# The block around the engines' instructions, and the order of elements in the forward width evictions

## The chip, the cores and the metric

One core of one Trainium2 chip. The metric is the device time of one execution in microseconds (us); the median of three runs stands for the kernel. TensorE (PE) multiplies matrices out of SBUF into PSUM, ScalarE (ACT) and VectorE (DVE) copy and transform, GpSimd (POOL) makes small vectors and issues some DMAs, SyncE (SP) issues most DMAs. The engines run on their own and meet only at semaphores.

## The reference

The input `x` is 2048 x 640 in bf16. It is normalised row by row, and two branches of the result are added to it.

```
xn = layernorm(x)                                  # over the 640
A  = irfft2( rfft2(xn) * (w_r + i w_i) )           # a spectral filter over both axes
B  = gelu(xn @ w1 + b1) @ w2 + b2                  # 640 -> 1536 -> 640
out = x + A + B
```

## The kernel before

**Branch B** is two dense layers on TensorE. The first layer's sums are evicted by ACT with the GELU (line 778) into `gT`; the second layer reads `gT` and `W2`. Their matmuls fill the time in which branch A waits for evictions.

**Branch A** writes the two-dimensional transform as matrix products with constant tables. In order: a fold of the rows on DVE, a transform over the first part of the long axis (PSUM into `XV`), the *forward width transform* (`XV` times `etab`, in six groups of two or three blocks, `GROUPS`), a small transform over the rest of the long axis (`Xb` times `mtab`, out into `Y`), the filter on DVE (`T`, `Z`, lines 845 and 849), and the same way back: `Z` times `ntab` into `U`, `T` or `gtab`, a DMA transpose into `XV`, the *inverse width transform* (`XV` times `getab`, out into `Wf`), an unfold on DVE (lines 900 and 905) and the last matmuls with `htab`, whose sums DVE adds up (line 961) and SyncE stores (line 964).

**The forward width transform** of a group with n blocks fills four PSUM banks: in each bank n runs of 160 sums, one bank for each of the four combinations of even and odd columns and of real and imaginary part. Two instructions evict them, v = 0 from the first two banks and v = 1 from the last two, into `Xb` as bf16. In `Xb` the sums of a block's two banks lie in turn, element by element: 320 neighbours from `v * (KP + 1)` on, with KP = 322. The helper `copy` emits an ACT activation (recorded at line 563) or a DVE copy (line 564). All matmuls are emitted by the helper at line 552.

**The order of the work** is written out by hand. `ORDER` lists for each engine the numbers of its operations one after another, and a planner (`Sched.schedule`) assigns PSUM banks and buffers along that list with a table of estimated costs. `Sched.sync` derives the semaphore waits that are needed, and `Sched.emit` gives each engine its list. The forward width transforms, the small transforms and the way back take turns in banks 0 to 3 (`ZONE`), the dense layers use banks 4 to 7.

**The emission** goes through a block: `nc.Block()` opens one, `block.sync(run("sp"))` and its four sisters each write one engine's instructions into a body of that block, and leaving the `ExitStack` closes it. On SyncE the list ends with waits for all stores (lines 440 to 442). The rows of the closing block are recorded at line 493, where the `with ExitStack()` of the kernel stands; those of the program's set-up at line 989.

Of the kernel before, what the change touches and what calls it, by code (L numbers as in the profile page):

```python
# [16 lines left out]
Q4 = 160  # L17
KP = 322
# [83 lines left out]
def dve_us(n, rate=1.0):  # L102
    return 0.066 + n / 960.0 / rate


def act_us(n, ptr=0):
    return 0.067 + n / 1200.0 + 0.078 * ptr
# [113 lines left out]
class Sched:  # L221
# [6 lines left out]
    def op(self, engs, prio, emit, reads=(), writes=(), after=(), rows=None, gate=(), alts=None, late=0.0):  # L228
        o = Op()
        o.name = writes[0].name if writes else ""  # L230
        o.engs, o.prio, o.emit = engs, prio, emit
        o.reads, o.writes, o.after = list(reads), list(writes), list(after)
        o.gate = gate if isinstance(gate, list) else list(gate)
        o.rows, o.late = rows, late
        o.nbytes = rows is not None
        o.alts, o.alt = alts, None
        o.seq = len(self.ops)
        o.eng, o.done, o.inc, o.count, o.sem = None, False, False, None, None
        o.deps = [w for b in o.reads for w in b.writers] + list(after)
        for b in o.reads:  # L240
            b.readers.append(o)
        for b in o.writes:
            b.writers.append(o)
        self.ops.append(o)
        return o
# [171 lines left out]
    def emit(self, es, last):  # L417
        nc = self.nc
        sems = {e: nc.alloc_semaphore(f"s_{e}") for e in self.engines if e != "sp"}
        for e in self.engines:  # L420
            n = 0
            for o in self.order[e]:
                if o.nbytes:
                    o.sem, o.count = nc.alloc_semaphore(f"d_{o.seq}"), 16
                elif o.inc:
                    n += 1
                    o.sem, o.count = sems[e], n
        block = es.enter_context(nc.Block())

        def run(name):  # L430
            def go(e):
                for o in self.order[name]:
                    for d in o.waits:
                        e.wait_ge(d.sem, d.count)
                    ins = o.emit(e, name) if o.alts is None else o.emit(e, o.alt)
                    if o.nbytes:
                        ins.then_inc(o.sem, 16)
                    elif o.inc:
                        ins.then_inc(o.sem, 1)
                if name == "sp":  # L440
                    for o in last:
                        e.wait_ge(o.sem, o.count)
            return go
        block.sync(run("sp"))
        block.gpsimd(run("pool"))
        block.vector(run("dve"))
        block.scalar(run("act"))
        block.tensor(run("pe"))


BLOCKS = [(0, 2), (2, 2), (4, 2), (6, 2), (8, 4), (12, 4)]
# [19 lines left out]
def bass_parallel_sum__spectral_gfnet__dense_activation_gelu__prompt_kernel(  # L471
# [21 lines left out]
    with ExitStack() as es:  # L493
        def sb(name, shape, dtype=BF):
            return es.enter_context(nc.sbuf_tensor(name, shape, dtype))

        def view(t, off, dims):
            width = int(np.prod(t.shape[1:]))
            return bass.AP(tensor=t, offset=off, ap=[[width, 128]] + dims)

        def part(t, p0, n, off, dims):
            width = int(np.prod(t.shape[1:]))
            return bass.AP(tensor=t, offset=p0 * width + off, ap=[[width, n]] + dims)
# [24 lines left out]
        xb3 = sb("Xb", [128, 6 * 2 * KP])  # L528
# [10 lines left out]
        def psb(slot, dims, off=0, p0=0, n=128):  # L539
            return bass.AP(tensor=PS, offset=p0 * 4096 + slot * 512 + off, ap=[[4096, n]] + dims)  # L540
# [15 lines left out]
        def pe(segs, prio, lst, **kw):  # L556

            return K.op([("pe", sum(u for _, u in segs))], prio, mms(lst), alts=[segs], **kw)

        def copy(dst, src, scale=1.0):  # L560
            def f(e, name):
                if name == "act":
                    return e.activation(dst(), src(), ACT.Copy, scale=scale)  # L563
                return e.tensor_copy(dst(), src())  # L564
            return f
# [32 lines left out]
        def load_w1(j, q="sp"):  # L598
# [6 lines left out]
             reads=[B_one], writes=[B_id])  # L605
# [62 lines left out]
        for c0, n in [(c, 1) for c in range(4)] + [(c, 2) for c in range(4, 16, 2)]:  # L668
            pr = 100 - c0 / 2
            B_mv, B_r = Buf(f"mv{c0}"), Buf(f"r{c0}")  # L670
            for c in range(c0, c0 + n):
                B_st = Buf(f"st{c}")
                for h in range(2):
                    st_op[c] = K.op([("dve", 0.393)], pr, lambda e, _, c=c, h=h: e.bn_stats(stats[:, c, 6 * h:6 * h + 6], view(X, c * D + H2 * h, [[1, H2]])),  # L674
                         reads=[B_x[c]], writes=[B_st], gate=mv_ops[:1])
# [3 lines left out]
                 reads=[B_mv, B_mh], writes=[B_r] + B_rs[a:b])  # L679

        for pair in range(8):
# [10 lines left out]
            for n in range(2):  # L692
# [5 lines left out]
                for d0, d1, bx in zip(cuts, cuts[1:], B_xs):  # L698
                    o = K.op([("dve", 0.066 + (d1 - d0) / 1980.0)], pr, lambda e, _, c=c, n=n, xnv=xnv, d0=d0, d1=d1: e.tensor_scalar(  # L699
                        out=xnv(n, d0, [[1, d1 - d0]]), in0=view(X, c * D + d0, [[1, d1 - d0]]), scalar1=mv[:, c, 0:1], scalar2=rstd[:, c:c + 1], op0=ALU.subtract, op1=ALU.mult),  # L700
                        reads=[B_x[c], B_rs[c]], writes=[xn, bx])
# [3 lines left out]
                if c in BYDMA:  # L705
                    ring_ops.append(K.op([("sp", 1.3)], 500, lambda e, _, c=c, n=n, xnv=xnv: e.dma_start_transpose(xnT[:, c, :, :], xnv(n, 0, [[1, D]])),
                         reads=[B_xn, xn], writes=[B_xnT[c]], rows=(40, 256)))
# [4 lines left out]
                for j0, j1, engs in ((0, 2, ["act"]), (2, 5, ["dve"])) if c < 2 else ((0, 5, ["dve", "act"]),):  # L712
# [8 lines left out]
                    if not c + j0:  # L721
# [5 lines left out]
                         reads=[tps], writes=[B_xnL[c][j0] if c < 2 else B_xnT[c]])  # L727
# [4 lines left out]
            for k, op in enumerate((ALU.add, ALU.subtract)):  # L732
                for o_, o0, o1, w in ((128 * k, 0, H2 - 1, 128), (512 + 32 * k, 128, H2 - 129, 32)):
                    ring_ops.append(K.op([("dve", dve_us(4 * w, 2))], pr, lambda e, _, op=op, x1v=x1v, xfv=xfv, o_=o_, o0=o0, o1=o1, w=w: e.tensor_tensor(  # L734
                        out=xfv(o_, [[D, 2], [2 * w, 2], [1, w]]), in0=x1v(o0, [[D, 2], [H2, 2], [1, w]]), in1=x1v(o1, [[D, 2], [H2, 2], [-1, w]]), op=op),
                        reads=[x1], writes=[xf]))
            aps = Buf(f"aps{pair}", psum, 3, ZONE["aps"])
            for n in range(2):
# [3 lines left out]
                    reads=[xf, B_g], writes=[aps])  # L742
                ring_ops.append(o)
                a_ops.append(o)
            for js in [[int(j) for j in g] for g in XASPLIT[pair].split()]:
# [3 lines left out]
                     reads=[aps], writes=[B_xa[pair]])  # L749
# [3 lines left out]
        for bi, (c0, nt) in enumerate(BLOCKS):  # L753
            for fc in range(NFC):
# [4 lines left out]
                if bi:  # L759
                    hps, at, part_ = Buf(f"hps{c0}_{fc}", psum, 1, ZONE["hps"]), 0, []  # L760
                    for js in ((0, 1, 2), (3, 4)):
                        part_ = [pe([("128", len(js) * mm_us(128 * nt))], pr + 0.01 * len(part_), lambda c0=c0, nt=nt, fc=fc, hps=hps, js=js: [
                            (psb(hps.slot, [[1, 128 * nt]]), view(W1, F * j + 128 * fc, [[1, 128]]), xnT[:, c0:c0 + nt, j, :], j == 0, j == 4) for j in js],
                            reads=B_w1s + B_xnT[c0:c0 + nt], writes=[hps], gate=part_)]
                        l1_ops += part_
                        l1_of.setdefault(bi, []).extend(part_)
                else:
                    at = 256 * (fc % 2)
                    if not at:
                        hps, part_ = Buf(f"hps0_{fc}", psum, 1, ANY), []  # L770
                        for j in range(5):
                            for t0, t1 in ((0, 1), (1, 2)) if j < LONE else ((0, 2),):
                                part_.append(pe([("128", 2 * mm_us(128 * (t1 - t0)))], pr + 8 - j - 2 * t0, lambda fc=fc, hps=hps, j=j, t0=t0, t1=t1: [
                                    (psb(hps.slot, [[1, 128 * (t1 - t0)]], 256 * h + 128 * t0), view(W1, F * j + 128 * (fc + h), [[1, 128]]), xnT[:, t0:t1, j, :], j == t0 == h == 0, j == 4) for h in range(2)],
                                    reads=[B_w1s[j]] + [B_xnL[t][j] for t in range(t0, t1)], writes=[hps], gate=part_[:1]))
# [4 lines left out]
                    reads=[hps, B_b1c], writes=[bg])  # L780
# [7 lines left out]
        def five(slot, n, lhs, tab):  # L788
            main, rem = width(slot, n, lhs, tab)
            return [(a, b, c, k % n == 0, False) for k, (a, b, c) in enumerate(main)] + [(a, b, c, False, True) for a, b, c in rem]  # L790

        def five_segs(n, far=0.0):
            return [("128", 4 * n * mm_us(Q4)), ("32", n * 0.07 + 0.02 + far)]
# [5 lines left out]
        for gi, (c0, n) in enumerate(GROUPS):  # L799
            xb = Buf(f"xb{gi}", p_xb)  # L800
            bps = Buf(f"bps{gi}", psum, 4, ZONE["bps"])
            pb_ops.append(pe(five_segs(n), PRIO["pb"] - c0 / 10, lambda c0=c0, n=n, bps=bps: five(
                bps.slot, n, lambda i, g, p0, k: part(XV, p0, k, 2048 * g + 128 * (c0 + i), [[1, 128]]), etab),
                reads=B_xa + [B_e], writes=[bps, xb]))
            for i in range(n):
                B_xb[c0 + i] = xb
                xb_at[c0 + i] = lambda xb=xb, i=i: (xb.slot * 3 + i) * 2 * KP
            for v in range(2):
                K.op([("dve", dve_us(320 * n) + 0.05), ("act", act_us(320 * n) + 0.08 * n)], PRIO["pb"] - c0 / 10,
                     copy(lambda v=v, xb=xb, n=n: view(xb3, xb.slot * 6 * KP + v * (KP + 1), [[2 * KP, n], [1, 2], [2, Q4]]),  # L810
                          lambda v=v, bps=bps, n=n: psb(bps.slot + 2 * v, [[Q4, n], [512, 2], [1, Q4]])), reads=[bps], writes=[xb])
        zone = {f"b{gi}": o for gi, o in enumerate(pb_ops)}
        for P in range(4):
            two = (2 * P, 2 * P + 1)
# [3 lines left out]
            for r in range(2):  # L818
# [6 lines left out]
                    reads=in_xb + [B_xbpad, B_m], writes=[cps])  # L825
# [16 lines left out]
            for pair, Y, TB, Z in zip(two, Ys, TBs, Zs):  # L842
                pr = PRIO["filt"] - pair / 5
                for k in range(2):
                    filt_ops.append(K.op([("dve", dve_us(4 * KP, 2))], pr, lambda e, _, k=k, Y=Y, TB=TB, pair=pair: e.tensor_tensor(  # L845
                        out=view(TT, TB.slot * 8 * KP + k * 4 * KP, [[2 * KP, 2], [KP, 2], [1, KP]]), in0=yv(Y, k == 1), in1=wv(pair, k), op=ALU.mult),
                        reads=[Y, B_wpad] + (B_w if pair == 7 else [B_w[k]]), writes=[TB], after=ring_ops))
# [4 lines left out]
            for v in range(2):  # L852
# [7 lines left out]
                for pp, U in enumerate(Us):  # L860
                    def evac(e, name, U=U, v=v, uv=uv, dps=dps, pp=pp):
                        for o_, w in ((0, 128), (512, 32)):
# [3 lines left out]
                         reads=[dps], writes=[U, B_us[pp]], after=a_ops + ring_ops)  # L866
# [10 lines left out]
        for q0, q1 in ((0, 12), (12, 16)):  # L877
            K.op([("dve", dve_us(128 * (q1 - q0))), ("act", act_us(128 * (q1 - q0)))], PRIO["eps"],
                 copy(lambda q0=q0, q1=q1: view(Yb, 8 * q0, [[128, 16], [1, 8 * (q1 - q0)]]), lambda q0=q0, q1=q1: view(XV, 4 * 2048 + 128 * q0, [[1, 16], [16, 8 * (q1 - q0)]])),
                 reads=B_v[q0:q1], writes=[B_xr], after=filt_ops)  # L880
# [7 lines left out]
        for gi, (c0, n) in enumerate(GROUPS):  # L888
# [5 lines left out]
                reads=B_v + [B_ge, B_xr], writes=[eps_], gate=[fin_ops[c0 - 5]] if c0 > 8 else [])  # L894
# [4 lines left out]
            for k, op in enumerate((ALU.add, ALU.subtract)):  # L899
# [3 lines left out]
                    reads=[yo], writes=[y2])  # L903
            for k, op in enumerate((ALU.add, ALU.subtract)):
# [3 lines left out]
                    reads=[y2], writes=[yf])  # L908
            for i in range(n):
# [26 lines left out]
                def second(c, fps, o0, w, pr, gate, base=base):  # L936
                    part_ = []
                    for f0 in range(0, NFC, 3):
# [8 lines left out]
                     reads=[xb2], writes=[xo], rows=(8, "acc"))  # L947
# [6 lines left out]
                for o0, w in [(0, D)] if c < 15 else [(0, H2), (H2, Q4), (H2 + Q4, Q4)]:  # L954
# [5 lines left out]
                        reads=[yf, B_h], writes=[fps, B_f], gate=part_ + ([l1_ops[-1]] if kept else []))  # L960
# [4 lines left out]
                                     reads=[os_, B_o], rows=(8, w * 2 if w * 2 in ROW_NS else 1280)))  # L965
# [38 lines left out]
```

## Time and profile before

| | |
|---|---|
| median of 3 runs | 147.75 us (147.56 to 147.98) |
| profiled execution, its own time | 148.03 us |
| its span, first to last recorded instruction | 146.1 us |
| PE busy / DVE / ACT / POOL | 140.2 / 112.7 / 80.9 / 23.7 us |
| granted TensorE clock | 1.0 |

The span is what the trace covers. The profiled execution's own time is 1.9 us longer; no row tells of that rest. In the rows below, a line begins with the kernel's line, the engine and the operation, then what is written and read, then how often, the busy time and the mean of one in ns; "idle before" and "<-" name what ended the wait. `PEld` is TensorE's weight load, which runs beside the matmuls. An engine's name with a q is its sequencer: waits, branches, drains and DMA issues, which do not count as busy.

### The profile page before, as it was taken

What the parts mean: (1) busy time and instruction counts of PE and PEld (TensorE: products, weight loads), DVE (VectorE), ACT (ScalarE), POOL (GpSimd) and SP (SyncE); (2) the same over time, 40 slices, a digit from 0 to 9 for tenths busy, and PEclk for the clock granted to TensorE, in tenths of its full rate; (3) what the DMA queues carried; (4) which work ended last, traced back from release to release, by engine and by line L of the source; (5) the groups of instructions that cost most, each with busy time, mean ns of one, the idle gap of its engine ahead of it and who ended that gap; (6) DMA issues with size and microseconds to landing.
All of it is one profiled execution on the core that took longest, in us unless ns stands there. A gap on an engine that the chain in (4) does not pass through costs nothing.

```text
span 146.1 us, 4081 instructions
## 1 busy us (share of the span) xinstructions
PE 140.2 (96%) x1702; PEld 90.8 (62%) x1720; DVE 112.7 (77%) x235; ACT 80.9 (55%) x145; POOL 23.7 (16%) x40
## 2 busy tenths in 40 slices
PE   7999999999999999999999999999999999999993
PEld 7788998888465455446544645554446666556572
DVE  1999999999844449789966967992422998998982
ACT  3208999999989769763555633216376755201000
POOL 2330302206100009220100120000063700000000
PEclk9999999999999999999999999999999999999999
DMA  4999999999997875949446571444559885103234
GB/s 110 320 407 354 320 132 303 150 182 241 283 162 149 193 192 123 235 99 180 94 92 121 63 154 30 40 110 94 90 116 230 175 202 180 45 4 137 90 135 135
DMA packets 30873, 23.63 MB, mean 162 GB/s; under 512 B 20488, under 2 KB 26888, under 8 KB 30728
## 3 DMA queue, kind: packets, MB, share of 16 engines
q1 hardware_dynamic: 28432, 17.81, 52.4%
q0 software_dynamic: 2368, 5.57, 17.4%
q8 instruction: 13, 0.21, 0.6%
q14 instruction: 4, 0.03, 0.1%
q10 hardware_dynamic: 56, 0.01, 0.0%
HBM read 13.55 MB, written 2.62 MB: 111 GB/s over the span
## 4 chain that ended last, share of the span: by engine, by line
PE 91%; DVE 4%; issue 2%; DMA 2%; POOL 0%
PE ps L552 90%; DVE stats L674 2%; DMA X<-in_A_x_dram 2%; DVE T L699 1%; DVE mv L676 0%; DVE xnT L564 0%; POOL rstd L678 0%; PE ps L718 0%; DVE W L961 0%
## 5 line engine op out<-in xcount | busy, mean ns | idle before, releaser
L552 PE MATMUL ps<-xnT,W 128*128 128x256 bf16 (+2 forms) x384 | 58.7, 300 | 0.2 <-DVE mv L676 0.2
L552 PE MATMUL ps<-W,gT 128*128 128x512 bf16 (+3 forms) x380 | 55.7, 292 | 1.6 <-issue 1.1
L552 PEld LDWEIGHTS ps<-W,gT 128*128 128x128 bf16 x396 | 30.3, 98 | 23.5 <-issue 1.6
L552 PEld LDWEIGHTS ps<-xnT,W 128*128 128x128 bf16 x384 | 33.3, 98 | 16.3 <-issue 1.6
L778 ACT ACTIVATE gT<-ps,b1col 128x256 bf16<-128x256 f32 (+1 forms) x72 | 35.3, 557 | 6.8 <-PE ps L552 6.5
L674 DVE BATCH_NORM_STATS2 stats<-X 128x6 f32<-128x320 bf16 x32 | 13.9, 475 | 2.2 <-DMA X<-in_A_x_dram 2.2
L563 ACT ACTIVATE Wf<-ps 128x960 bf16<-128x960 f32 (+1 forms) x8 | 7.0, 901 | 13.5 <-PE ps L552 13.5
L946 POOL DMA_DIRECT2D X<-in_A_x_dram x8 | 7.1, 1067 | 40.1 <-DMA Wf<-in_A_w_r_dram 17.6
L845 DVE TENSOR_TENSOR T<-Y,Wf 128x1288 bf16<-128x1288 bf16 x16 | 12.7, 826 | 0.0
L946 POOL DMA_DIRECT2D xnT<-in_A_x_dram x8 | 7.4, 1151 | 25.3 <-ACT xnT L928 25.3
L678 POOL TENSOR_TENSOR rstd<-mv,mhalf 128x2 f32<-128x2 f32 (+1 forms) x10 | 7.2, 715 | 26.8 <-DVE mv L676 26.7
L563 ACT ACTIVATE Xb<-ps 128x960 bf16<-128x960 f32 (+1 forms) x7 | 7.7, 1102 | 6.8 <-PE ps L552 6.8
L564 DVE CAST Y<-ps 128x644 bf16<-128x644 f32 x8 | 6.5, 828 | 5.5 <-PE ps L552 5.5
L563 ACT ACTIVATE XV<-ps 128x1280 bf16<-128x1280 f32 (+3 forms) x10 | 9.5, 961 | 0.7 <-PE ps L552 0.7
L564 DVE CAST Xb<-ps 128x960 bf16<-128x960 f32 (+1 forms) x5 | 5.9, 1176 | 4.1 <-PE ps L552 4.1
L734 DVE TENSOR_TENSOR T<-T 128x512 bf16<-128x512 bf16 (+1 forms) x32 | 8.5, 311 | 0.0
L699 DVE TENSOR_SCALAR T<-X,mv,rstd 128x640 bf16<-128x640 bf16 (+2 forms) x17 | 7.1, 430 | 0.9 <-POOL rstd L678 0.6
L900 DVE TENSOR_TENSOR Wf<-Wf 128x960 bf16<-128x960 bf16 (+1 forms) x12 | 7.0, 597 | 0.5 <-ACT Wf L563 0.3
L961 DVE TENSOR_TENSOR W<-ps,X 128x640 bf16<-128x640 f32 x8 | 6.5, 820 | 1.1 <-PE ps L552 1.1
L849 DVE TENSOR_TENSOR Z<-T 128x644 bf16<-128x644 bf16 x16 | 7.1, 487 | 0.1
L961 DVE TENSOR_TENSOR W<-ps,xnT 128x640 bf16<-128x640 f32 (+2 forms) x10 | 6.7, 685 | 0.7 <-PE ps L552 0.7
L552 PE MATMUL ps<-etab,XV 32*128 32x160 bf16 (+1 forms) x128 | 7.2, 232 | 0.0
(55 smaller groups left out, 132.3 us busy)
## 6 DMA issues: line engine op xcount, KB each, us to landing
X<-in_A_x_dram POOLq DMA_DIRECT2D x8, 320.0 KB, 4.8
xnT<-in_A_x_dram POOLq DMA_DIRECT2D x8, 320.0 KB, 5.0
out_dram<-W SPq DMA_DIRECT2D x15, 160.0 KB, 1.8
X<-in_A_x_dram SPq DMA_DIRECT2D x7, 320.0 KB, 7.5
W<-in_B_w_dram SPq DMA_DIRECT2D x5, 384.0 KB, 6.1
W<-in_B_w_dram SPq DMA_DIRECT2D x4, 480.0 KB, 7.5
Wf<-in_A_w_i_dram SPq DMA_DIRECT2D x6, 160.5 KB, 5.8
Wf<-in_A_w_r_dram SPq DMA_DIRECT2D x6, 160.5 KB, 4.1
```

Source lines behind the costliest of these rows:

```text
L552: ins = e.matmul(o_, lhsT=lw, rhs=rh, start=st, stop=sp_, skip_group_check=True)
L563: return e.activation(dst(), src(), ACT.Copy, scale=scale)
L564: return e.tensor_copy(dst(), src())
L674: st_op[c] = K.op([("dve", 0.393)], pr, lambda e, _, c=c, h=h: e.bn_stats(stats[:, c, 6 * h:6 * h + 6], view(X, c * D + H2 * h, [[1, H2]]) ...
L678: K.op([("pool", 0.65)], 500, lambda e, _, a=a, b=b: e.tensor_tensor(out=rstd[:, a:b], in0=mv[:, a:b, 1], in1=mhalf[:, a:b], op=ALU.pow), ...
L699: o = K.op([("dve", 0.066 + (d1 - d0) / 1980.0)], pr, lambda e, _, c=c, n=n, xnv=xnv, d0=d0, d1=d1: e.tensor_scalar(out=xnv(n, d0, [[1, d1 ...
L734: ring_ops.append(K.op([("dve", dve_us(4 * w, 2))], pr, lambda e, _, op=op, x1v=x1v, xfv=xfv, o_=o_, o0=o0, o1=o1, w=w: e.tensor_tensor(ou ...
L778: K.op([("act", act_us(128 * nt, 1))], pr + PRIO["gelu"] + GP[bi], lambda e, _, c0=c0, nt=nt, fc=fc, hps=hps, at=at: e.activation(gT[:, fc ...
L845: filt_ops.append(K.op([("dve", dve_us(4 * KP, 2))], pr, lambda e, _, k=k, Y=Y, TB=TB, pair=pair: e.tensor_tensor(out=view(TT, TB.slot * 8 ...
L849: K.op([("dve", dve_us(2 * KP, 2))], pr, lambda e, _, TB=TB, Z=Z, r=r, op=op: e.tensor_tensor(out=view(Zb, Z.slot * 4 * KP + r * KP, [[2 * ...
L946: xo_ops[c] = K.op([("pool", 0.9)], 51 - c / 20, lambda e, _, c=c, xov=xov: e.dma_start(xov(0, D), xv[:, c, :], accum_op=ALU.add), reads=[ ...
L961: K.op([("dve", dve_us(w))], 95, lambda e, _, os_=os_, fps=fps, o0=o0, w=w, xov=xov, base=base: e.tensor_tensor(out=view(W1, OST + os_.slo ...
```

## The change

It has two parts. In `Sched.emit` no block is opened: each engine's list is emitted into the program itself, in the same order as before. And the evictions of the forward width transforms walk their elements in another order: the two innermost dimensions of the access patterns change places, in the read and in the write. Before, such an instruction reads 160 neighbours from one bank, then 160 from the other, and writes every second element of `Xb`; after, it reads one element from each of two banks in turn and writes neighbours. The values and where they land are the same, and so are the cost estimates and `ORDER`.

```diff
@@ Sched.emit
-        block = es.enter_context(nc.Block())
...
-        block.sync(run("sp"))
-        block.gpsimd(run("pool"))
-        block.vector(run("dve"))
-        block.scalar(run("act"))
-        block.tensor(run("pe"))
+        run("sp")(nc.sync)
+        run("pool")(nc.gpsimd)
+        run("dve")(nc.vector)
+        run("act")(nc.scalar)
+        run("pe")(nc.tensor)
@@ the evictions of the forward width transforms
             for v in range(2):
                 K.op([("dve", dve_us(320 * n) + 0.05), ("act", act_us(320 * n) + 0.08 * n)], PRIO["pb"] - c0 / 10,
-                     copy(lambda v=v, xb=xb, n=n: view(xb3, xb.slot * 6 * KP + v * (KP + 1), [[2 * KP, n], [1, 2], [2, Q4]]),
-                          lambda v=v, bps=bps, n=n: psb(bps.slot + 2 * v, [[Q4, n], [512, 2], [1, Q4]])), reads=[bps], writes=[xb])
+                     copy(lambda v=v, xb=xb, n=n: view(xb3, xb.slot * 6 * KP + v * (KP + 1), [[2 * KP, n], [2, Q4], [1, 2]]),
+                          lambda v=v, bps=bps, n=n: psb(bps.slot + 2 * v, [[Q4, n], [1, Q4], [512, 2]])), reads=[bps], writes=[xb])
```

## The prediction

> **What bounds the kernel now.** I read the page's first two parts, then the chain that ended last, then the waits of the matmul stream between 12.4 and 143.5 us, and last the two places that the change touches: the rows of the end, and those of the evictions into `Xb`.
>
> ```profile
> span 146.1 us, 4081 instructions
> PE 140.2 (96%) x1702; PEld 90.8 (62%) x1720; DVE 112.7 (77%) x235; ACT 80.9 (55%) x145; POOL 23.7 (16%) x40
> PEclk9999999999999999999999999999999999999999
> ```
>
> TensorE is busy for 96% of the span, at the full granted clock throughout (a 9 is 90% or more). The chain says the same with an order in time:
>
> ```profile
> 12.36 38.28 PE ps L552 x391
> ...
> 140.59 2.98 PE ps L552 x31
> 143.56 0.02 issue
> 143.58 0.32 DVE W L961
> ```
>
> From 12.36 to 143.56 us the chain never leaves TensorE. What is left over is a head of 12.4 us, in which the first rows are loaded and normalised, and a tail of 2.5 us, in which the last tile is evicted and stored. The waits of the matmuls between 12.4 and 143.5 us are one line:
>
> ```profile
> PE ps L552 <- issue: 1.3, 8, 0.2
> ```
>
> Eight gaps, 1.3 us together, and none of them was ended by ACT, DVE or a DMA. So in the middle of this kernel no eviction is late for TensorE. An eviction that gets shorter there buys nothing; one that gets longer costs what it exceeds its slack by.
>
> **The block.** The change emits the same instructions of each engine in the same order, without the block around them. The trace has rows for what closes the block, all on line 493, and for SyncE's last waits for the stores, on line 442:
>
> ```profile
> L442 SPq EVENT_SEMAPHORE  x9: 17/28/28, 144.5 to 145.6; - x9
> L493 SPq COMPARE_BRANCH  x1: 41/41/41, 145.7 to 145.7; - x1
> L493 SPq DRAIN  x1: 7/7/7, 145.8 to 145.8; - x1
> L493 POOLq EVENT_SEMAPHORE  x2: 17/17/17, 145.9 to 145.9; - x2
> L493 SPq EVENT_SEMAPHORE  x1: 17/17/17, 146.0 to 146.0; - x1
> L493 PEldq EVENT_SEMAPHORE  x1: 51/51/51, 146.0 to 146.0; - x1
> L493 DVEq DRAIN  x1: 361/361/361, 143.6 to 143.6; - x1
> ```
>
> Read in order of time: the last wait for a store starts at 145.6; SyncE branches at 145.7 and drains at 145.8; GpSimd counts the engines and releases them at 145.9; each engine takes the release at 146.0, and TensorE's row of 51 ns ends the span at 146.1. DVE's drain began at 143.6 and the other engines had been there before SyncE too: this is a chain of SyncE and GpSimd alone, with nothing beside it. Without the block the span should end with the last wait for a store (the one that the branch carries becomes one more row of some 28 ns), at about 145.7: 146.1 - 145.7 = **0.4 us off the span**, with 0.1 of rounding in the rows.
>
> The block's opening has no rows to lose. The barrier ahead of it comes from the program's set-up (line 989, not 493), and the kernel's first work starts right behind it:
>
> ```profile
> L989 SPq EVENT_SEMAPHORE  x1: 17/17/17, 0.7 to 0.7; - x1
> 0.81 0.87 SPq L547 DMA_DIRECT2D X<-in_A_x_dram  x2
> ```
>
> That barrier stays, so I put the opening at nothing. If something unseen lay between 0.7 and 0.81 us, it could give back 0.1 us at most.
>
> Outside the span lie 148.03 - 146.1 = 1.9 us of the profiled execution, of which no row tells anything. Four engines will have finished their last instruction 1.7 us or more before SyncE (the last of them DVE, whose drain ended at 144.0), where before all five left the barrier within a tenth; if the program's end gathers the engines again, they will be there already. The bounds are nothing and a good part of the 1.9 us. I take 0.05, nearer to nothing, by the row nearest to it: TensorE's 51 ns as the last to leave the barrier, which SyncE would no longer have to stand behind. The sum is made against the profiled execution: 148.03 - 0.4 - 0.05 = 147.58. That execution was 148.03 - 147.75 = 0.28 us over the median of the three runs, and I carry that as a constant: 147.75 - 0.45 = **147.3 us**.
>
> **The evictions.** Twelve instructions (two of each of six groups, seven on ACT, five on DVE) copy a transform out of four banks into `Xb` as bf16. Before, each reads 160 neighbours of one bank and writes every second element; after, it reads one element of each of two banks in turn and writes neighbours. Same elements, same engines, same place in each queue, no wait added. The nearest rows:
>
> ```profile
> L563 ACT ACTIVATE Xb<-ps 128x960 bf16<-128x960 f32 x4 | 5.0, 1253 | 5.0 <-PE ps L552 5.0
> L563 ACT ACTIVATE Wf<-ps 128x960 bf16<-128x960 f32 x6 | 5.6, 968 | 5.4 <-PE ps L552 5.4
> L563 ACT ACTIVATE Xb<-ps 128x640 bf16<-128x640 f32 x3 | 2.7, 901 | 1.8 <-PE ps L552 1.8
> L563 ACT ACTIVATE Wf<-ps 128x640 bf16<-128x640 f32 x2 | 1.4, 698 | 8.1 <-PE ps L552 8.1
> L564 DVE CAST Xb<-ps 128x960 bf16<-128x960 f32 x4 | 5.0, 1250 | 2.5 <-PE ps L552 2.5
> L564 DVE CAST Wf<-ps 128x960 bf16<-128x960 f32 x2 | 2.3, 1154 | 0.0
> L564 DVE CAST Wf<-ps 128x640 bf16<-128x640 f32 x2 | 1.6, 824 | 2.8 <-PE ps L552 2.8
> L564 DVE CAST Xb<-ps 128x640 bf16<-128x640 f32 x1 | 0.9, 880 | 1.6 <-PE ps L552 1.6
> ```
>
> The `Wf` rows are the inverse transform's evictions: the same read of runs of 160, a write of neighbours. Against them the stepped write costs ACT 285 ns at 960 elements and 203 at 640, DVE 96 and 56. If the read in turn is free, the twelve save 4 x 0.285 + 3 x 0.203 = 1.75 us of ACT and 4 x 0.096 + 0.056 = 0.44 us of DVE. None of it lies on the path, by the line of TensorE's waits above: worth 0.
>
> Whether the read in turn is free no row shows. The nearest are the evictions of the inverse column transform (`U`, `T`, `gtab`), which read every second element of a bank, against `XV`, which reads neighbours:
>
> ```profile
> L563 ACT ACTIVATE U<-ps 128x512 bf16<-128x512 f32 x5 | 3.0, 597 | 5.8 <-PE ps L552 5.8
> L563 ACT ACTIVATE XV<-ps 128x512 bf16<-128x512 f32 x3 | 1.8, 614 | 0.7 <-PE ps L552 0.7
> L564 DVE CAST T<-ps 128x512 bf16<-128x512 f32 x3 | 2.1, 692 | 3.8 <-PE ps L552 3.8
> L564 DVE CAST XV<-ps 128x512 bf16<-128x512 f32 x1 | 0.7, 681 | 0.0
> ```
>
> 597 against 614 ns and 692 against 681: a step in the read costs neither engine anything. A hop to another bank is farther than a step, so this bears on it without proving it. I take it as free, with half the read rate as the other end. Half rate is 1.03 ns more per element on DVE, (1154 - 824) / 320, and 0.84 on ACT, (968 - 698) / 320: a DVE eviction of 960 would take 1.154 + 0.99 = 2.14 us against 1.25, and of 640 1.48 against 0.88. The Trainium skill (Vector Engine (DVE) Microarchitecture Reference, section 5.2 Measured stream behaviour on trn2) speaks against the change: it has a port stream at full rate only in runs of at least two neighbouring four-byte words, and gives 1.73 ns per column against 1.054 where one source hops at every element. By that figure, an estimate, an eviction of 960 on DVE would take 1.80 us and the sum would come to about 148.2 us. It is stated for SBUF, and the stepped reads above, which have no two neighbours either, do not agree with it.
>
> **Rivals.** *The read in turn is slow* (slower). TensorE's next use of the banks or of `Xb` follows three evictions closely:
>
> ```profile
> 48.54 0.88 DVE L564 CAST Xb<-ps 128x640 bf16<-128x640 f32 x1 [1.59 <-PE ps L552]
> 49.60 0.49 PE L552 MATMUL ps<-Xb,mtab 32*32 32x322 bf16 x32
> 54.64 1.25 DVE L564 CAST Xb<-ps 128x960 bf16<-128x960 f32 x1 [1.03 <-PE ps L552]
> 56.09 0.58 PE L552 MATMUL ps<-Xb,mtab 32*32 32x322 bf16 x32
> 67.56 1.24 DVE L564 CAST Xb<-ps 128x960 bf16<-128x960 f32 x1
> 69.00 1.31 PE L552 MATMUL ps<-etab,XV 128*128 128x160 bf16 x24
> ```
>
> The slack is 49.60 - 49.42 = 0.18, 56.09 - 55.89 = 0.20 and 69.00 - 68.80 = 0.20 us. With e ns more per element than now, TensorE stands still for 0.64e - 0.18, 0.96e - 0.20 and 0.96e - 0.20 there, 2.56e - 0.58 in all, and every matmul behind is fixed in order and moves with it. The block's 0.45 us is eaten at e = 0.40, an eviction of 960 taking 1.63 us; the change is slower by over 0.3% from about e = 0.57. At half rate e is 0.93 ((2.14 - 1.25) / 0.96): 1.80 us of standing still, 147.3 + 1.8 = 149.1 us. For it: single elements from two banks occur nowhere in this trace, and the stepped write shows that an access without neighbours can cost. Against it: the stepped reads. Chance 0.20, of which 0.18 comes out slower and 0.02 within 0.3%.
>
> *The shorter evictions do reach TensorE.* The weight load behind the first of those evictions stood idle longer than the same load with nothing to wait for:
>
> ```profile
> 49.60 0.19 PEld L552 LDWEIGHTS ps<-Xb,mtab 32*32 32x32 bf16 x32 [0.42 <-ACT Xb L563]
> 51.38 0.19 PEld L552 LDWEIGHTS ps<-Xb,mtab 32*32 32x32 bf16 x32 [0.26 <-issue]
> ```
>
> If the difference of 0.16 us is a stall that the modelled ends of the matmuls cover up, it goes: 147.3 - 0.16 = 147.14 us. Against it: no such gap among the matmuls. Chance 0.10, faster.
>
> *The barrier was free.* If what follows the span waits for something else, the 1.9 us grow by what the span loses, and the change does nothing: 147.75 us. For it: what fills the 1.9 us is not to be seen. Against it: the rows of line 493 wait for nothing but each other. Chance 0.10, same.
>
> **How the numbers follow.** 0.3% of 147.75 is 0.44 us, about what a measurement of this kernel can tell from no change. My forecast, chance 0.60, is 147.3 us, 0.45 below: on the edge. Its span part is 0.3 to 0.5 by rounding, and the part outside can only add to it; I put 0.44 of the 0.60 at faster and 0.16 at same. Faster: 0.44 + 0.10 = 0.54. Same: 0.16 + 0.10 + 0.02 = 0.28. Slower: 0.18. The range starts at 146.8 (0.4 off the span and 0.55, over a quarter, off what lies outside it; beyond that 0.05) and reaches to 148.4, e = 0.65 in the slow case (2.56 x 0.65 - 0.58 = 1.08 over 147.3), which leaves out some 0.10 of it. The forecast's own range is 146.8 to 147.45.
>
> **What would show it.** Right: no rows of line 493 at the end, a span of about 145.7, the last row a wait of SyncE; `Xb` evictions at about 0.97 and 0.70 us on ACT, 1.15 and 0.82 on DVE; still no gap among the matmuls from 12.4 to 143.5. Wrong: `Xb` rows above 1.6 us with the matmuls at 49.60, 56.09 and 69.00 late, or a last matmul that is not near 143.3; a span shorter by 0.4 with an unchanged time would speak for the free barrier.

## The result and the profile after

The kernel with the change takes 146.81 us (median of 22 runs), the kernel before 147.94 (22 runs): a ratio of 0.9925, 95% interval 0.9907 to 0.9943, 1.1 us faster. The forecast was 147.3 us, range 146.8 to 148.4: the right side, and about two and a half times the size that I had given it (0.45 us). The profiled execution after took 147.13 us, its span 145.9. So 1.2 us lie outside the span, where before there were 1.9. In the experiments below one run, of the barrier put back, was slow (149.83 us at a granted clock of 0.988), and that kernel's figures leave it out.

The end, by the rows of one line, as before (engine, operation, count, duration in ns, first and last start in us). It is SyncE's wait for the stores:

```profile
L441 SPq EVENT_SEMAPHORE  x9: 27/28/28, 144.7 to 145.8; - x9
```

With this row the span ends; the branch, the drains and the hand-over through GpSimd are gone, as forecast. The last wait stands later than before's (145.6), because TensorE stood still once in this execution between 12.4 and 143.5 us. The waits of the matmuls in that stretch:

```profile
PE ps L551 <- DVE X L951: 0.6, 1, 0.6
```

And the chain that ended last, around that place (start, length, what):

```profile
54.43 5.81 DMA X<-in_A_x_dram
...
60.33 0.84 DVE X L951
61.17 0.05 issue
61.22 82.59 PE ps L551 x1043
```

An accumulating load of `x` landed late, DVE's sum behind it ended late, and TensorE waited 0.6 us for it. The profile of the same program run again, in the experiments below, does not have this wait. Two kernels that differ from it at their end alone have it again (0.4 us where GpSimd waits for the stores, 0.9 where DVE does). So it comes and goes with the execution, and is not what the change does. The eight gaps of before ("issue", 1.3 us) are missing here, and this page has 1720 matmuls where before's had 1702, for the same 1720 weight loads:

```profile
PE 141.5 (97%) x1720; PEld 90.3 (62%) x1720; DVE 112.3 (77%) x235; ACT 79.6 (55%) x145; POOL 23.9 (16%) x40
```

So those eight gaps look like 18 matmuls without a record rather than waits, and the profiles below bear it out. The whole change run again has 1702 matmuls and the eight gaps; the kernel in which ACT alone waits for the stores has 1720 and none. From the first `gtab` matmul to the last matmul the one takes 127.23 us (16.13 to 143.36) and the other 127.21 (15.71 to 142.92). The evictions (groups by form; mean ns of one behind the comma):

```profile
L562 ACT ACTIVATE Xb<-ps 128x960 bf16<-128x960 f32 x4 | 3.9, 972 | 5.3 <-PE ps L551 5.2
L562 ACT ACTIVATE Xb<-ps 128x640 bf16<-128x640 f32 x3 | 2.1, 703 | 2.0 <-PE ps L551 2.0
L563 DVE CAST Xb<-ps 128x960 bf16<-128x960 f32 x4 | 4.6, 1158 | 2.6 <-PE ps L551 2.5
L563 DVE CAST Xb<-ps 128x640 bf16<-128x640 f32 x1 | 0.8, 825 | 1.7 <-PE ps L551 1.7
```

972, 703, 1158 and 825 ns, against the 968, 698, 1154 and 824 of the `Wf` rows before: the stepped write's price is gone, and the read from two banks in turn costs 1 to 5 ns of some 700 to 1160, next to nothing on either engine.

What had to be found out: which part of the change brings the 1.1 us, and why 0.7 of them lie where no row tells anything. *Time outside* below is a run's own time less its span, as a median over its runs. It is a steady number: 1.21 to 1.30 us over the 22 runs after, 1.84 to 2.06 over 24 runs of the kernel before on one chip, while the spans of either kernel vary by more than a microsecond.

### The profile page after: what moved, and what is told of

It is laid out like the page before. It is cut to its first block, busy times and chain, and to the rows that moved or that the text cites. A ratio compares the mean times of both kernels' runs of the same rounds, so it can differ in the third digit from the quotient of the medians.

```text
span 145.9 us, 4087 instructions
## 1 busy us (share of the span) xinstructions
PE 141.5 (97%) x1720; PEld 90.3 (62%) x1720; DVE 112.3 (77%) x235; ACT 79.6 (55%) x145; POOL 23.9 (16%) x40
## 4 chain that ended last, share of the span: by engine, by line
PE 80%; DMA 8%; SPq 6%; DVE 3%; issue 1%; ACT 0%; DVEq 0%
PE ps L551 80%; DMA X<-in_A_x_dram 6%; SPq L705 3%; SPq L546 3%; DMA Wf<-in_A_w_r_dram 3%; DVE stats L673 1%; PE ps L717 1%; DVE X L951 1%; DVE T L733 0%; DVE mv L675 0%; DVE XV L563 0%; ACT xnT L562 0%; DVE W L960 0%; DVE T L698 0%; DVEq L433 0%
## 5 line engine op out<-in xcount | busy, mean ns | idle before, releaser
L551 PE MATMUL ps<-W,gT 128*128 128x512 bf16 (+3 forms) x396 | 58.7, 295 | 0.6 <-DVE X L951 0.6
L562 ACT ACTIVATE Xb<-ps 128x960 bf16<-128x960 f32 (+1 forms) x7 | 6.0, 856 | 7.3 <-PE ps L551 7.3
L951 DVE TENSOR_TENSOR X<-ps,X 128x640 f32<-128x640 f32 x8 | 6.5, 821 | 1.4 <-DMA X<-in_A_x_dram 1.1
L562 ACT ACTIVATE Y<-ps 128x644 bf16<-128x644 f32 x8 | 5.7, 708 | 3.0 <-PE ps L551 3.0
L562 ACT ACTIVATE U<-ps 128x512 bf16<-128x512 f32 (+1 forms) x10 | 3.8, 434 | 6.3 <-PE ps L551 6.3
```

The lines of the kernel that those rows point to most:

```text
L551: ins = e.matmul(o_, lhsT=lw, rhs=rh, start=st, stop=sp_, skip_group_check=True)
L951: kept_ops.append(K.op([("dve", dve_us(D))], 30, lambda e, _, kps=kps, xov=xov: e.tensor_tensor(out=xov(0, D), in0=psb(kps.slot, [[1, D]]) ...
```

## The experiments

**One part at a time.** The first kernel leaves out the new order of the evictions, the second keeps the block, the third is the whole change again; all on one chip, beside the same 24 runs of the kernel before.

```diff
 # e1: the change, with the evictions of before
-  [[2 * KP, n], [2, Q4], [1, 2]]   <-  [[Q4, n], [1, Q4], [512, 2]]
+  [[2 * KP, n], [1, 2], [2, Q4]]   <-  [[Q4, n], [512, 2], [1, Q4]]
 # e2: the kernel before, with the evictions of the change
-  [[2 * KP, n], [1, 2], [2, Q4]]   <-  [[Q4, n], [512, 2], [1, Q4]]
+  [[2 * KP, n], [2, Q4], [1, 2]]   <-  [[Q4, n], [1, Q4], [512, 2]]
```

> No block, evictions as before. Theory 1 (all of the gain is the block's closing: 0.36 us of rows at the end of the span, and some 0.7 us outside the span, which fell from 1.98 to 1.26 us): about 1.0 to 1.1 us under the kernel before, ratio 0.993, time outside the span about 1.25 us, last row a wait of SyncE. Theory 2 (the shorter evictions carry part of it): clearly less than the whole change, 0.36 us or so, ratio 0.997 to 0.998.

> The evictions in the new order, the block kept. Theory 1: no change beyond noise, ratio 0.999 to 1.001, although the Xb rows fall to 0.97 and 0.70 us on ACT and 1.16 and 0.82 on DVE; time outside the span still 1.9 to 2.0 us. Theory 2: 0.3 to 0.7 us faster, ratio 0.995 to 0.998.

> The whole change again, as the yardstick on this chip. Both theories: ratio about 0.9925; under theory 1 the same as the kernel without the block alone, under theory 2 faster than it by 0.3 us or more.

| | time, us | ratio, 95% interval | span | time outside |
|---|---|---|---|---|
| kernel before | 147.80 | | 145.90 | 1.92 |
| no block only | 146.72 | 0.9927 (0.9895 to 0.9959) | 145.50 | 1.25 |
| evictions only | 147.90 | 1.0001 (0.9981 to 1.0021) | 145.85 | 1.96 |
| whole change | 146.69 | 0.9909 (0.9875 to 0.9942) | 145.45 | 1.25 |

The block is the whole gain: 0.40 us of span and 0.67 outside it. The evictions alone bring nothing, though their rows fall just as in the whole change. The groups of the kernel with the evictions alone, and its matmul waits from 12.4 to 143.5 us:

```profile
L563 ACT ACTIVATE Xb<-ps 128x960 bf16<-128x960 f32 x4 | 3.9, 972 | 5.3 <-PE ps L552 5.2
L564 DVE CAST Xb<-ps 128x960 bf16<-128x960 f32 x4 | 4.6, 1159 | 2.6 <-PE ps L552 2.5
```

```profile
PE ps L552 <- issue: 1.3, 8, 0.2
```

Both engines are done earlier, and TensorE, which never waited for them, goes on as it did. Theory 2 falls. The weight load that the prediction suspected of a hidden stall, here at 49.37 us, still stands idle for 0.42 us behind the shorter eviction, as it did behind the longer one, so that idle time was not the eviction's.

**The barrier without the block.** If the four engines that were held back make the time outside, a barrier alone brings it back; if it is the branch to the block's end, it does not.

```diff
         run("pe")(nc.tensor)
+        nc.all_engine_barrier()
```

> The whole change, and behind every engine's list one barrier of all engines, without a block: the drains and semaphores of the old end are back, the branch to the end of the block is not. Theory 1a (the 0.7 us outside the span were lost because the barrier held four engines back, which now reach the program's end early): rows of the end back, some 0.25 to 0.35 us more span, and the time outside back at 1.9 to 2.0 us; ratio 0.999 to 1.0. Theory 1b (SyncE's branch to the end of the block cost it, since what follows a branch has to be fetched): outside the span stays near 1.25 us; ratio about 0.995.

147.73 us, ratio 0.9992 (0.9969 to 1.0015), time outside 2.01 us. The span is 145.60 us, only 0.15 over the whole change where 0.25 to 0.35 had been expected. There is no branch in it, nor a block that is opened, and the whole gain is gone: theory 1b falls.

**Who must not be late.** Is it the barrier's own instructions, or the lateness of the engines behind it? In the first kernel all five engines wait for the stores with plain waits; in the others one engine alone waits, and SyncE is done after its last issue.

```diff
-                if name == "sp":
+                if name in LATE_END:        # all five; then ("pool",), ("act",), ("pe",), ("dve",)
                     for o in last:
                         e.wait_ge(o.sem, o.count)
```

> The whole change, and every engine, not SyncE alone, waits at its end for the stores. No barrier, no drain, no branch, but all five engines reach the program's end together, at about 145.7 us of the span. Theory 1a (early arrival is what saves the time outside): outside the span 1.8 to 2.0 us, time near 147.4. Theory 1c (it is the barrier's own instructions, a drain or a semaphore left to be settled, that cost it): outside the span 1.25 us, time near 146.8.

> The whole change, but GpSimd alone waits for the stores, SyncE reaches its end after its last issue. Theory 1a, with one engine's program end dearer than SyncE's: if it is GpSimd's, 1.7 to 2.0 us outside the span; if not, 1.0 to 1.3. Theory 1c: 1.25 whichever engine waits.

> The whole change, but ACT alone waits for the stores. Theory 1a: 1.7 to 2.0 us outside the span if ACT's program end is the dear one, else 1.0 to 1.3. Theory 1c: 1.25.

> The whole change, but TensorE alone waits for the stores. Theory 1a: 1.7 to 2.0 us outside the span if TensorE's program end is the dear one (its barrier row of 51 ns is the longest), else 1.0 to 1.3. Theory 1c: 1.25.

> The whole change, but DVE alone waits for the stores. By theory 1a each engine has its own price between its last row and the program's end (SyncE 1.25, ACT 1.41, TensorE 1.52, GpSimd 1.79 us); DVE's should lie with ACT's and TensorE's, 1.4 to 1.6 us outside the span. If it is near 1.9, it is DVE and not GpSimd that the old barrier held up.

| engine that ends last | time outside, us (lowest to highest run) | time, us | ratio, 95% interval |
|---|---|---|---|
| SyncE (the change) | 1.25 (1.21 to 1.27) | 146.69 | 0.9909 (0.9875 to 0.9942) |
| DVE | 1.36 (1.32 to 1.39) | 146.79 | 0.9921 (0.9886 to 0.9955) |
| ACT | 1.41 (1.38 to 1.47) | 146.79 | 0.9930 (0.9900 to 0.9960) |
| TensorE | 1.52 (1.49 to 1.54) | 147.01 | 0.9987 (0.9915 to 1.0060) |
| GpSimd | 1.79 (1.76 to 1.84) | 147.14 | 0.9949 (0.9929 to 0.9970) |
| all five | 1.73 (1.70 to 1.80) | 147.07 | 0.9952 (0.9937 to 0.9967) |

The times are medians of 4 to 8 runs, and TensorE's interval is too wide to order it by its ratio; the time outside, which varies less from run to run, orders them better. GpSimd and all five overlap, and DVE's highest run (1.39) lies above ACT's lowest (1.38). The rows also come from three chips: SyncE's from that of the first experiments, DVE's from a third, the other four from a second. The kernel before had 1.92 us outside on the first two and 2.04 on the third, so DVE's place beside ACT is not shown. Beside SyncE it is: on that third chip the last kernel below, which ends on SyncE, left 1.27 us outside (1.24 to 1.32). The ends of the kernels with all five and with GpSimd alone, by the rows of their waits:

```profile
L444 ACTq EVENT_SEMAPHORE  x9: 38/38/38, 144.1 to 145.4; - x9
L444 POOLq EVENT_SEMAPHORE  x9: 43/43/43, 144.1 to 145.4; - x9
L444 DVEq EVENT_SEMAPHORE  x9: 49/50/50, 144.1 to 145.4; - x9
L444 PEldq EVENT_SEMAPHORE  x9: 51/51/51, 144.1 to 145.4; - x9
L444 SPq EVENT_SEMAPHORE  x9: 28/28/28, 144.3 to 145.4; - x9
```

```profile
L444 POOLq EVENT_SEMAPHORE  x9: 43/43/43, 144.0 to 145.4; - x9
```

In both the last wait starts at 145.4 and the span ends with it, so what differs from SyncE's case is what follows. I read it so: each engine has something of its own to do between its last row and the end of the measured time, and the one that is done last is waited for. What that something is, no row tells. SyncE's is the shortest, GpSimd's 0.54 us longer. All five late cost about as much as GpSimd alone (1.73 against 1.79; 1.8 to 2.0 had been expected): the others hide behind it. The old barrier made GpSimd late, and that is up to 0.54 of the 0.67 us. Theory 1a stands, theory 1c falls for this part.

**The rest of 0.13 us and more.** The barrier left 1.92 us outside in the kernel before, plain waits of all five 1.73 on the same chip. The rows make the rest larger: GpSimd's last row in the kernel before starts at 145.9, ahead of the span's end at 146.1, and 1.79 us from there reach to 147.7 of the 148.03 that the execution took. By that estimate GpSimd's lateness leaves some 0.3 us of the time outside unexplained. Do the drains make the difference?

```diff
         run("pe")(nc.tensor)
+        nc.all_engine_barrier(sem_only=True)
```

> The whole change with a barrier of all engines at the end that has the semaphores but no drains. All five engines waiting for the stores without a barrier left 1.73 us outside the span, the barrier with drains 2.01. If the drains make the difference: 1.7 to 1.8. If the barrier's semaphores do: 1.9 to 2.0.

```profile
L448 SPq EVENT_SEMAPHORE  x2: 17/22/28, 145.6 to 145.8; - x2
L448 POOLq EVENT_SEMAPHORE  x2: 17/17/17, 145.7 to 145.7; - x2
```

147.85 us, ratio 0.9991 (0.9954 to 1.0027), time outside 2.06 us (1.78 to 2.18), beside 2.04 of the kernel before on the same chip: the drains are not it. That leaves the barrier's semaphores or the order in which they let the engines go; which of the two stays open.

**The slack of the evictions.** The prediction had three evictions with some 0.2 us to spare, and a formula for what a longer one costs. No run so far had a longer one, so this kernel makes them longer by the write:

```diff
-  [[2 * KP, n], [2, Q4], [1, 2]]   <-  [[Q4, n], [1, Q4], [512, 2]]
+  [[2 * KP, n], [1, Q4], [Q4, 2]]  <-  [[Q4, n], [1, Q4], [512, 2]]
```

> The whole change, but the evictions, which still read from two banks in turn, write each element 160 away from the last: two runs side by side instead of neighbours, so the columns of Xb are in another order and what is computed from them differs. A test of the write's price and of the slack. If only neighbours are cheap: Xb rows at 1.25 us or more (960 elements) and 0.90 or more (640), as in the kernel before. Up to 1.25 us the time is that of the whole change, 146.8. With e ns per element beyond the kernel before, TensorE should stand still for 0.64e - 0.18, 0.96e - 0.20 and 0.96e - 0.20 us at the three tight evictions. A theory in which every eviction counts in full would add 2.56e us or more, and already some 0.3 us at 1.25.

168.14 us, ratio 1.1357 (1.1328 to 1.1386). The evictions' groups, DVE's rows in order of time, and the matmuls behind them, with what ended their idle time:

```profile
L562 ACT ACTIVATE Xb<-ps 128x960 bf16<-128x960 f32 x4 | 17.7, 4422 | 6.8 <-PE ps L551 6.8
L562 ACT ACTIVATE Xb<-ps 128x640 bf16<-128x640 f32 x3 | 9.1, 3021 | 1.5 <-PE ps L551 1.3
L563 DVE CAST Xb<-ps 128x960 bf16<-128x960 f32 x4 | 17.6, 4404 | 4.4 <-PE ps L551 4.4
```

```profile
51.53 2.98 DVE L563 CAST Xb<-ps 128x640 bf16<-128x640 f32 x1 [1.16 <-PE ps L551]
61.22 4.40 DVE L563 CAST Xb<-ps 128x960 bf16<-128x960 f32 x1 [2.01 <-PE ps L551]
78.83 4.40 DVE L563 CAST Xb<-ps 128x960 bf16<-128x960 f32 x1
```

```profile
50.52 0.96 PE L551 MATMUL ps<-etab,XV 128*128 128x160 bf16 x16 [2.54 <-ACT Xb L562]
54.62 0.50 PE L551 MATMUL ps<-Xb,mtab 32*32 32x322 bf16 x32 [1.95 <-ACT Xb L562]
65.79 0.50 PE L551 MATMUL ps<-Xb,mtab 32*32 32x322 bf16 x32 [3.05 <-ACT Xb L562]
...
83.31 2.28 PE L551 MATMUL ps<-etab,XV 128*128 128x160 bf16 x24 [2.88 <-DVE Xb L563]
90.44 0.50 PE L551 MATMUL ps<-Z,ntab 32*32 32x320 bf16 x32 [1.75 <-DVE Z L848]
...
102.28 0.50 PE L551 MATMUL ps<-xnT,W 128*128 128x256 bf16 x3 [1.11 <-ACT gT L777]
105.59 0.60 PE L551 MATMUL ps<-xnT,W 128*128 128x512 bf16 x2 [2.00 <-ACT gT L777]
```

The three tight places stood still for 1.95, 3.05 and 2.88 us. By the formula they should have for (2.98 - 0.88) - 0.18 = 1.92, (4.40 - 1.25) - 0.20 = 2.95 and (4.40 - 1.24) - 0.20 = 2.96. The slacks read from before's rows hold to 0.1 us. (At the first two places the row names ACT's eviction of the same group; it runs beside DVE's and is as long, 2.99 and 4.42 us.) For the whole time the formula is far too small. It gives 7.8 us; the kernel is 21.4 us slower than the whole change. With evictions as long as these, the first group with its larger slack (2.54 us) and work queued behind the evictions on ACT and DVE (the last three rows, 4.86 us) come on top. And the matmuls themselves ran longer: the profile of the whole change, then this one's, with its granted clock in 40 slices:

```profile
PE 139.4 (96%) x1702; PEld 90.1 (62%) x1720; DVE 112.4 (77%) x235; ACT 79.5 (55%) x145; POOL 23.7 (16%) x40
```

```profile
PE 146.6 (87%) x1702; PEld 92.8 (55%) x1720; DVE 127.2 (75%) x235; ACT 99.7 (59%) x145; POOL 24.0 (14%) x40
PEclk9999999999999698799879999789999999999999
```

The clock was 0.90 on the mean from 46 to 112.3 us, the stretch with the gaps, and 1.00 ahead of it and behind it. The named gaps (15.3 us) and the 7.2 us more of matmul time make 22.5 of the 22.9 us between the two spans (145.7 and 168.6). Why the clock fell there no run shows.

## Why the prediction was right, and which term was too small

**The rows at the end**: 0.4 us off the span, with the last wait for a store as its last row. Measured 0.40 (145.90 to 145.50, no block only). Right, by the mechanism given.

**Outside the span**: this is the step that was mis-sized. I took 0.05 us, "by the row nearest to it", TensorE's 51 ns as the last to leave the barrier; measured 0.67. I had the mechanism for the larger part of it (four engines are at the program's end already when SyncE comes; some 0.13 to 0.3 us are the open rest above) and priced it by a row of the barrier itself, which says nothing of what follows the barrier. What follows differs by engine, from 1.25 us for SyncE to 1.79 for GpSimd, and GpSimd was done at 121.6 us of the span before it was held back: its drain started at 115.2 and took 6.4 us, in the rows of the kernel before.

```profile
L493 POOLq DRAIN  x1: 6442/6442/6442, 115.2 to 115.2; - x1
```

The bound above, "a good part of the 1.9 us", was the better reading; it is what kept 146.8 in the range. That the measured 146.81 lies inside is luck all the same: the range allowed 0.55 us outside the span, less than the 0.67, and the kernel before measured 0.19 us slower over 22 runs than over the three that the range was built on. The same program took 146.69 on the chip of the first experiments. The Trainium skill (Runtime: NRT & Kernel Launch, section The ~15µs preamble/postamble breakdown) lists a meeting of all engines of about 1.5 us behind the kernel. The 1.25 to 1.79 us here lie around that figure, though they also hold whatever is measured ahead of the first row; that the two are the same thing no run here shows.

**The block's opening**: nothing. The chain after begins with the first load at 0.81 us, as the load was issued before, and a barrier at the end alone, without a block, takes the whole gain away.

```profile
0.81 2.27 DMA X<-in_A_x_dram
```

**The evictions**: read in turn free, durations of the `Wf` rows, worth 0. Right on all three (972 against 968 ns, 1158 against 1154; ratio 1.0001 alone). The figure of the Trainium skill (Vector Engine (DVE) Microarchitecture Reference, section 5.2 Measured stream behaviour on trn2), 1.73 against 1.054 ns for a source that hops at every element, does not carry over to this read from PSUM: 1.04 ns per element on DVE, (1158 - 825) / 320, with a hop at each. The same section also tells of a one-source operation whose read alternates between two regions at every element at the full read rate, writing one word for two read; that is nearer to this read, and the trace agrees with it.

**The rivals**: the slow read did not come. Its price formula held for the three gaps when the write was made slow, and left out 13 to 14 us of what the slow write cost in all. The shorter evictions do not show at TensorE: the whole change and the change without them are 146.69 and 146.72 us, well inside their intervals, and the idle time of 0.42 us at the suspected weight load did not change. The free barrier is refuted from both sides, by its removal and by putting it back.

## What to carry to other kernels

An engine's last instruction is not the end of its cost. Let the engine whose program end is short (here SyncE) be the one that waits for the last stores, let the others run out as early as they can, and put no barrier of all engines behind that wait. Before shortening an eviction, read the slack of the matmul behind it: in a stream without gaps 1.7 us of ACT time, 4 x 0.281 + 3 x 0.198, are worth nothing. The same slack told to a tenth of a microsecond how long that matmul stands still behind a longer eviction, but not what a much longer one costs the kernel: here 7.8 us by the slacks and 21.4 measured.

## What the runs showed of the hardware that I had not expected

- Measured time outside the span, with one engine alone in coming last: SyncE 1.25 us, DVE 1.36, ACT 1.41, TensorE 1.52, GpSimd 1.79 (each with whatever lies ahead of the first row, and from three chips).
- A bf16 write that hops 320 bytes at every element takes 4.4 ns per element on ACT and on DVE alike, (4422 - 3021) / 320, where the write that stepped over every second element took 1.1 on ACT, (1253 - 901) / 320, and 1.2 on DVE, (1250 - 880) / 320, and neighbours 0.84 on ACT, (972 - 703) / 320. It does so with one engine alone as with both at once: the two evictions of the last group, one after the other on ACT, take 3.07 and 3.00 us, and the one that runs beside DVE's 2.99. Reads that hop from bank to bank at every element cost next to nothing (972 against 968 ns on ACT, 1158 against 1154 on DVE).
